# A softplus MLP in chunks of four f tiles with all tokens inside, its low weight parts on VectorE, and one gather earlier

## The chip, the cores and the metric

The kernel runs on one core of one Trainium2 chip. The metric is the device time of one execution in microseconds (us); lower is better. TensorE is called PE here, VectorE DVE, ScalarE ACT, GpSimd POOL and SyncE SP. PE runs its matmuls in order, and every engine works through its own queue in program order: the kernel is built with a manual schedule, so the order of the Python calls is the order on each engine.

## The reference

Three stages follow one another: attention in which a query sees only keys of its own hash bucket, a mixture of experts (one expert for each token), and a dense MLP with softplus. Cut to what matters:

```python
def _attn_ref(q, k, v, proj):                  # B, H, S, D = 2, 8, 768, 64
    mask = bucket(q @ proj)[..., :, None] == bucket(k @ proj)[..., None, :]
    scores = np.where(mask, scale * q @ k.T, -1e9)
    return softmax(scores) @ v

def _moe_ref(x, modality_id, w_gate, modality_bias, w1, w2):   # N, D, E, F = 1536, 512, 8, 1024
    e_idx = argmax(x @ w_gate + modality_bias[modality_id])
    for e in range(E):
        out[e_idx == e] = gate_w * (relu(x[e_idx == e] @ w1[e]) @ w2[e])

def _moe2_ref(x, w_in, w_out):                 # d_model, d_ff = 512, 2048
    h = x @ w_in
    g = np.maximum(h, 0.0) + np.log1p(np.exp(-np.abs(h)))
    return g @ w_out
```

The weights of the last stage come as 8-byte floats; they are read as pairs of 32-bit words.

## The kernel before

**Arithmetic.** Every large product is made of three matmuls on a high and a low part: xH·wH, xL·wH and xH·wL. The high part is a copy rounded to the matmul's type (made by ACT), the low part the rest (a subtraction of two tiles). So each weight tile costs one ACT copy and one subtraction.

**Experts.** `pipe` runs 16 slots of 128 tokens, each with one expert's weights. For slot s, `gather(s)` (an indirect DMA issued by POOL) fetches the rows of the slot's tokens, `xT` transposes them on PE, `g1` and `g2` are the two products, and `yout` scales the result on ACT and scatters it, with an indirect DMA of POOL's, into `x2_dram`, sorted by expert. The weight splits (`split_hi` on ACT, `split_lo` on DVE, L1000) run up to four tiles ahead of PE. `gather(1)` and `gather(2)` are issued in `route_b`, and `gather(s + 2)` for s from 1 on at the head of `pipe`'s slot s, behind the routing work that POOL has queued. The first part of the experts overlaps the end of attention by a hand-written order: `DRAIN` holds three strings of short names, one for PE, one for ACT, one for DVE and POOL, and `do` turns each name into a call (`b2` is `route_b(2)`, `Y` is `yout(0)`, `d1` is `route_d(1)`).

**Overflow.** Behind slot 16 stands a block under `tc.If` (L1206) for rare slot counts; in these runs it is not entered, and POOL settles the semaphores of the scatters that it skips.

**Second MLP.** The 2048 hidden units are 16 f tiles of 128. Weights of tile f: `wload` (two DMAs on SP into one of two buffers `wraw`), `wconv` (three DVE operations, L1276, L1278, L1280, that make 4-byte floats of the pairs), `wsplit` (high part on ACT, L1289; low part on POOL, L1290). Tokens: `x2load` brings 128 rows of `x2_dram` (from tile 4 on by SP's queue, two buffers), `x2prep` transposes them on PE (L1252) and splits them into x2H and x2L. The 12 token tiles are three groups g of four. `mlp1(g, f)` is 12 matmuls (L1301), then on ACT Abs, Exp and Ln, then on DVE gg (L1309), gH and gL (L1318). `mlp2(g, f)` is another 12 matmuls (L1336): four token tiles, three each, into four PSUM banks `ps_o`. On PE the order is mlp1 of a step, then mlp2 of the step before.

The loop in `mlp` is g outside and f inside: the 16 f tiles of group 0, in whose steps all weights are converted and split just in time (`jit`), then 16 of group 1, then 16 of group 2 with the weights kept in SBUF. PSUM sums over all f; after f = 15 each token tile is copied out (L1342 on ACT, L1344 on DVE) and scattered to the output by POOL (L1345). The token tiles of group g+1 are loaded and prepared in the last four steps of group g. The last six f of group 2 (`NLATE`) run mlp1 first and then all of mlp2 token tile by token tile, so that the output starts early. The step (0, 0), and the first weights (f = 0, 1, 2), are done inside the experts, from a hook of `pipe`: `wsplit(0)` and `wsplit(1)` behind slots 5 and 9, `wsplit(2)` and mlp1(0, 0) in the last slot.

Of the kernel before, what the change touches and what calls it, by code (L numbers as in the profile page):

```python
# [479 lines left out]
class Moe:  # L480
# [651 lines left out]
    def pipe(self, a, b, hook):  # L1132

        if a > 1:
            self.order(a, b)
            for _ in range(3):
                self.split()
            self.xT(a)
        for s in range(a, b + 1):
            if a + 2 <= s + 2 < b:  # L1140
                self.gather(s + 2)
            if s < b:
                for c in range(4):
# [71 lines left out]
    def open_mlp_early(self, ctx):  # L1215
        tc = self.tc
        kw = dict(reuse_waits="tile")
        self.wwa = ctx.enter_context(tc.tile_pool(name="wwa", bufs=1, **kw))
        self.gp = ctx.enter_context(tc.tile_pool(name="gp", bufs=2, **kw))
        self.x2_p = ctx.enter_context(tc.tile_pool(name="x2_p", bufs=2, **kw))  # L1220
        self.sA = ctx.enter_context(ExitStack())
        self.wraw = self.sA.enter_context(tc.tile_pool(name="wraw", bufs=2, **kw))
        self.mw, self.x2, self.x2t, self.oidx, self.mraw, self.m32 = {}, {}, {}, {}, {}, {}
        self.early = [0, 1, 2]
        self.NLATE = 6

    def open_mlp(self, ctx):
        kw = dict(reuse_waits="tile")
        self.wwb = ctx.enter_context(self.tc.tile_pool(name="wwb", bufs=1, side="right", **kw))
        self.po = ctx.enter_context(self.tc.tile_pool(name="po", bufs=4, space=PSUM, **kw))  # L1230

    def x2load(self, j):
        t = self.x2_p.tile([P, self.D + 1], F32, tag="x2", name="x2")
# [5 lines left out]
    def x2prep(self, j):  # L1239
        nc = self.nc  # L1240
        g, i = divmod(j, 4)
        if i == 0:
            if g == 1:
                self.sA.close()
                self.x2b = self.sA.enter_context(self.tc.tile_pool(name="x2b", bufs=1, reuse_waits="tile"))
            pool = self.x2b if g == 1 else self.x2_p
            self.x2t[g] = [pool.tile([P, self.KD, 512], F32R, tag="x2" + n, name="x2" + n, bufs=1) for n in "HL"]
        H, L = self.x2t[g]
        x = self.x2.pop(j)
        ps = self.pt.tile([P, self.KD, P], F32, tag="pt", name="ps_x2")  # L1250
        for k in range(self.KD):
            nc.tensor.transpose(ps[:, k], x[:, k * P:(k + 1) * P], self.ident)  # L1252
        sl = slice(i * P, (i + 1) * P)
        nc.scalar.copy(H[:, :, sl], ps)
        nc.vector.tensor_tensor(L[:, :, sl], ps, H[:, :, sl].bitcast(F32), op=ALU.subtract)
        if i == 0:
            self.oidx[g] = self.x2_p.tile([P, 4], I32, tag="oidx", name="oidx", bufs=3)
        (nc.vector if g == 1 and i < 2 else nc.gpsimd).tensor_copy(self.oidx[g][:, i:i + 1], x[:, self.D:])
# [24 lines left out]
    def wsplit(self, f):  # L1283
        nc = self.nc
        w = self.m32.pop(f).bitcast(F32)
        pool = self.wwa if f in self.early else self.wwb
        H = pool.tile([P, 2, 512], F32R, name=f"mwH{f}")
        L = pool.tile([P, 2, 512], F32R, name=f"mwL{f}")
        nc.scalar.copy(H, w)  # L1289
        nc.gpsimd.tensor_tensor(L, w, H.bitcast(F32), op=ALU.subtract)  # L1290
        self.mw[f] = (H, L)

    def mlp1(self, g, f):
        nc = self.nc
        H, L = self.mw[f]
        xH, xL = self.x2t[g]
        ps = self.py.tile([P, 512], F32, tag="py", name="ps_f")
        for k in range(self.KD):
            sl = slice(k * P, (k + 1) * P)
            for n, (w, x) in enumerate(((H, xH), (H, xL), (L, xH))):  # L1300
# [2 lines left out]
        nc.scalar.activation(a, ps, AF.Abs)  # L1303
        nc.scalar.activation(a, a, AF.Exp, scale=-1.0)
        nc.scalar.activation(a, a, AF.Ln, bias=1.0)  # L1305
        jit = not g and f > 0
        conv = self.wconv(f + 3, nc.vector) if jit and f + 3 < self.NF else iter(())
        gg = self.gp.tile([P, 512], F32, tag="gg", name="gg")
        nc.vector.scalar_tensor_tensor(gg, ps, 0.0, a, op0=ALU.max, op1=ALU.add)  # L1309
        late = g == self.TT // 4 - 1 and f >= self.NF - self.NLATE  # L1310
        gH, gL = (self.x2b.tile([P, 512], F32R, name=f"g{n}{f}") if late else self.gp.tile([P, 512], F32R, tag=f"g{n}", name=f"g{n}")
                  for n in "HL")
        if g:
            nc.vector.tensor_copy(gH, gg)
        else:
            nc.scalar.copy(gH, gg)
        next(conv, None)
        nc.vector.tensor_tensor(gL, gg, gH.bitcast(F32), op=ALU.subtract)  # L1318
        next(conv, None)
        if jit and f + 2 < self.NF:  # L1320
            self.wsplit(f + 2)
        next(conv, None)
        if jit and f + 5 < self.NF:
            self.wload(f + 5)
        return gH, gL

    def mlp2(self, g, f, gH, gL, tiles=range(4)):
        nc = self.nc
        H, L = self.mw[f]
        NF = self.NF  # L1330
        if f == 0:
            self.ops = [self.po.tile([P, self.D], F32, tag="po", name="ps_o") for _ in range(4)]
        for i in tiles:
            sl = slice(i * P, (i + 1) * P)
            for n, (a, w) in enumerate(((gH, H), (gH, L), (gL, H))):
                nc.tensor.matmul(self.ops[i], a[:, sl], w[:, 1], start=(f == 0 and n == 0), stop=(f == NF - 1 and n == 2))  # L1336
            if f == NF - 1:
                if i == 0:
                    self.osb = self.gp.tile([P, 4, self.D], F32, tag="osb", name="osb", bufs=1)
                o = self.osb[:, i]  # L1340
                if i % 2:
                    nc.scalar.copy(o, self.ops[i])  # L1342
                else:
                    nc.vector.tensor_copy(o, self.ops[i])  # L1344
                nc.gpsimd.indirect_dma_start(out=self.out, in_=o, in_offset=None,  # L1345
                                             out_offset=bass.IndirectOffsetOnAxis(ap=self.oidx[g][:, i:i + 1].bitcast(U32), axis=0),
                                             bounds_check=self.N - 1, oob_is_err=False)

    def mlp(self):
        NF = self.NF  # L1350
        pend = self.pend
        NG = self.TT // 4
        for g in range(NG):
            for f in range(NF):
                if g + 1 < NG:
                    if NF - 4 <= f < NF - 2:
                        self.x2load(4 * (g + 1) + f - (NF - 4))
                    elif f >= NF - 2:
                        j = 4 * (g + 1) + 2 * (f - (NF - 2))
                        self.x2prep(j)  # L1360
                        self.x2prep(j + 1)
                        if f == NF - 2:
                            self.x2load(j + 2)
                            self.x2load(j + 3)
                if g == NG - 1 and f == 0:
                    self.sA.close()
                    self.x2b = self.sA.enter_context(self.tc.tile_pool(name="late", bufs=1, reuse_waits="tile"))
                if (g, f) != (0, 0):
                    pend.append((g, f) + self.mlp1(g, f))
                if len(pend) > 1 and (g < NG - 1 or f < NF - self.NLATE + 1):  # L1370
                    self.mlp2(*pend.pop(0))

        last = [(i, x) for i in range(4) for x in pend]
        n = len(pend)
# [15 lines left out]

# [3 lines left out]
)  # L1394

# [2 lines left out]
def kernel(ctx, tc, q, k, v, proj, mid, wg, mb, w1, w2, win, wout, out):  # L1398
# [6 lines left out]
    with tc.manual_schedule():  # L1405
# [4 lines left out]
        with ExitStack() as c0:  # L1410
# [51 lines left out]
            def do(k):  # L1462
# [53 lines left out]
                    moe.hT_pe(0, *n, bank(att.ps_t, "t"))  # L1516
                elif a in "QR":
                    (moe.hT_hi if a == "Q" else moe.hT_lo)(0, *n)
                elif a == "Y":
                    moe.yout(0)  # L1520
                elif a == "z":
# [99 lines left out]
```

## Time and profile before

| | us |
|---|---|
| median of 3 runs | 782.02 (781.60 to 782.22) |
| the profiled execution, whole | 782.45 |
| its span on the core | 780.7 |
| PE busy | 756.3 (97%) |
| DVE busy | 585.2 (75%) |
| ACT busy | 520.5 (67%) |
| POOL busy | 284.0 (36%) |

Times of rows are us from the span's start. The page's busy share is an average: attention takes the first 270 us, the experts run to about 494 us, the second MLP from there to the end. The stages have to be read one by one. A matmul's shown duration overlaps that of its neighbours, so 12 matmuls of about 0.4 us each take 2.8 us, and PE's pace is better read from starts than from its busy share.

### The profile page before, as it was taken

The page shows a single profiled execution, that of the slowest core. Times are in us where ns is not written, and L with a number is a line of the kernel's source. Part 1 is how long each engine was busy: PE and PEld are TensorE (multiplying, and loading weights), DVE is VectorE, ACT ScalarE, POOL GpSimd, SP SyncE. Part 2 cuts the span into 40 slices and gives each one's busy share as a digit, 9 for nine tenths or more (in the row PEclk, how much of TensorE's full clock was granted, in tenths as well). Part 3 has the DMA queues.
Part 4 walks back from the last instruction along what each step waited for, and adds up shares of the span by engine and source line. Part 5 has one row for each costly group of instructions (what it writes and reads, how often), then busy time and mean ns, then how long its engine had stood idle before and what let it go on. Part 6 is the DMA issues. An engine that isn't in the chain of part 4 may idle for free.

```text
span 780.7 us, 13124 instructions
## 1 busy us (share of the span) xinstructions
PE 756.3 (97%) x4231; PEld 644.5 (83%) x4232; DVE 585.2 (75%) x845; ACT 520.5 (67%) x869; POOL 284.0 (36%) x624
## 2 busy tenths in 40 slices
PE   8899999999999998999999999999989999999996
PEld 6899999999999866878878878776668888888874
DVE  6898888988988797999998988799983323433250
ACT  5788787887879677898898988545554333342340
POOL 4555544446565475233342153544441100020001
PEclk9999999999999999999999999999999999999999
DMA  7845636636570014579963642334431000010001
GB/s 187 192 126 126 163 88 164 150 70 169 176 206 22 21 42 144 212 237 349 373 234 107 217 139 80 117 121 162 162 108 52 27 1 1 27 55 1 0 1 54
DMA packets 72601, 95.28 MB, mean 122 GB/s; under 512 B 31842, under 2 KB 48226, under 8 KB 72528
## 3 DMA queue, kind: packets, MB, share of 16 engines
q1 hardware_dynamic: 67152, 83.85, 36.1%
q0 software_dynamic: 3744, 9.45, 3.4%
q10 hardware_dynamic: 1632, 1.08, 0.5%
q8 instruction: 35, 0.57, 0.3%
q14 instruction: 38, 0.31, 0.1%
HBM read 105.18 MB, written 10.76 MB: 148 GB/s over the span
## 4 chain that ended last, share of the span: by engine, by line
PE 73%; DVE 9%; DMA 8%; issue 4%; POOL 3%; ACT 2%; ACTq 0%; POOLq 0%; DVEq 0%; SPq 0%
PE ps_o L1336 12%; PE ps_f L1301 12%; PE ps_o L310 9%; PE ps_y L1116 8%; PE s L253 8%; PE ps_t L286 8%; PE ps_g L1069 7%; DMA x_dram<-y,cpi 6%; DVE w L1280 3%; PE s L332 2%; DVE w L1278 2%; PE ps_prep L184 2%; PE ps_ht L1087 1%; PE ps_prep L178 1%; DVE gL L1318 1%
## 5 line engine op out<-in xcount | busy, mean ns | idle before, releaser
L1000 DVE TENSOR_TENSOR wL<-wr,wH 128x1024 fp32r<-128x1024 f32 (+1 forms) x137 | 162.7, 1218 | 13.1 <-ACT wH L995 12.8
L995 ACT CAST wH<-wr 128x1024 fp32r<-128x1024 f32 (+1 forms) x144 | 141.3, 1005 | 8.3 <-PE ps_g L1069 3.1
L1309 DVE SCALAR_TENSOR_TENSOR gg<-ps_f,ga 128x512 f32<-128x512 f32 x48 | 33.0, 688 | 108.0 <-ACT ga L1305 108.0
L263 DVE TENSOR_REDUCE mx<-s 128x1 f32<-128x768 f32 x96 | 91.5, 954 | 21.6 <-PE s L332 18.9
L274 ACT ACTIVATE p<-s,nb,sc 128x768 f32<-128x768 f32 x96 | 95.9, 999 | 15.6 <-POOL nb L265 12.8
L296 DVE TENSOR_TENSOR PL<-ps_t,PH 128x512 fp32r<-128x512 f32 x144 | 98.2, 683 | 6.8 <-ACT PH L291 6.3
L1303 ACT ACTIVATE ga<-ps_f 128x512 f32<-128x512 f32 x48 | 28.6, 597 | 108.0 <-PE ps_f L1301 107.9
L291 ACT CAST PH<-ps_t 128x512 fp32r<-128x512 f32 x144 | 83.7, 587 | 16.0 <-PE ps_t L286 13.4
L253 PE MATMUL s<-K,Q 76*128 76x384 f32 (+1 forms) x384 | 89.0, 353 | 2.4 <-ACT K L239 1.5
L310 PE MATMUL ps_o<-PH,vhl 128*128 128x256 f32 x288 | 86.8, 317 | 0.3 <-ACT Os L316 0.3
L286 PE MATMUL ps_t<-ident,p 128*128 128x128 f32 x576 | 86.3, 272 | 0.4 <-DVE PL L296 0.4
L1301 PE MATMUL ps_f<-x2H,mwL 128*128 128x512 f32 x192 | 76.7, 400 | 3.4 <-POOL mwL L1290 3.4
L1301 PE MATMUL ps_f<-x2H,mwH 128*128 128x512 f32 x192 | 76.3, 398 | 0.6 <-PEq L1206 0.6
L1336 PE MATMUL ps_o<-mwH,gL 128*128 128x512 f32 x192 | 76.8, 400 | 0.0
L1336 PE MATMUL ps_o<-mwH,gH 128*128 128x512 f32 x192 | 75.8, 395 | 0.0
L1336 PE MATMUL ps_o<-mwL,gH 128*128 128x512 f32 x192 | 75.8, 395 | 0.0
L1301 PE MATMUL ps_f<-x2L,mwH 128*128 128x512 f32 x192 | 75.5, 393 | 0.0
L286 PEld LDWEIGHTS ps_t<-ident,p 128*128 128x128 f32 x576 | 69.4, 141 | 2.3 <-PE s L253 0.7
L1290 POOL TENSOR_TENSOR mwL<-w,mwH 128x1024 fp32r<-128x1024 f32 x16 | 47.3, 2959 | 62.7 <-ACT mwH L1289 57.3
L310 PE MATMUL ps_o<-PL,vhl 128*64 128x256 f32 x288 | 68.3, 280 | 0.0
L253 PEld LDWEIGHTS s<-K,Q 76*128 76x128 f32 (+1 forms) x384 | 63.5, 191 | 4.3 <-ACT p L274 2.1
L1128 POOL DMA_INDIRECT x_dram<-y,cpi x17 | 25.1, 1476 | 100.1 <-ACT y L1123 63.2
(293 smaller groups left out, 1655.2 us busy)
## 6 DMA issues: line engine op xcount, KB each, us to landing
wr<-in_moe_w_dram SPq DMA_DIRECT2D x136, 512.0 KB
wraw<-in_moe_w_in_dram SPq DMA_DIRECT2D x16, 512.0 KB
wraw<-in_moe_w_out_dram SPq DMA_DIRECT2D x16, 512.0 KB
Q<-qH SPq DMA_DIRECT2D x28, 192.0 KB
K<-kH SPq DMA_DIRECT2D x28, 192.0 KB
rawv<-in_v_dram SPq DMA_DIRECT2D x8, 384.0 KB
x_dram<-x SPq DMA_DIRECT2D x8, 384.0 KB
rawq<-in_q_dram SPq DMA_DIRECT2D x14, 192.0 KB
```

Source lines behind the costliest of these rows:

```text
L253: self.nc.tensor.matmul(s[:, h, :HS], d[l, j][:kk, ts], d[r, j][:kk, h * HS:(h + 1) * HS], start=(a == 0), stop=(a == 1))
L263: nc.vector.tensor_reduce(mx, s[:, :, :self.HS], axis=AX.XY, op=ALU.max)
L274: self.nc.scalar.activation(e["P"][ti].rearrange("p (h c) -> p h c", h=2), s[:, :, :self.HS], AF.Exp, scale=sc, bias=nb, accum_out=e["sum" ...
L286: self.nc.tensor.transpose(ps[:, kk, t], e["P"][t][:, kt * P:(kt + 1) * P], self.ident)
L291: self.nc.scalar.copy(e["PH"][:, 2 * bk:2 * bk + 2].rearrange("p k n -> p (k n)"), e["T", bk])
L296: self.nc.vector.tensor_tensor(e["PL"][:, sl].rearrange("p k n -> p (k n)"), e["T", bk], e["PH"][:, sl].rearrange("p k n -> p (k n)").bitc ...
L310: self.nc.tensor.matmul(O[:n, :2 * P], vh[:, j, kt, :n], e[nm][:, kt], start=(kt == 0 and n == P), stop=(kt == NT - 1 and n == P))
L995: self.nc.scalar.copy(self.wt[s, c][0][:, sl], self.raw[c][:, sl])
L1000: eng.tensor_tensor(L[:, sl], self.raw[c][:, sl], H[:, sl].bitcast(F32), op=ALU.subtract)
L1116: nc.tensor.matmul(ps, a[:, f], ww[:, w], start=(f == 0 and n == 0), stop=(f == self.KF - 1 and n == 2))
L1301: nc.tensor.matmul(ps, w[:, 0, sl], x[:, k], start=(k == 0 and n == 0), stop=(k == self.KD - 1 and n == 2))
L1336: nc.tensor.matmul(self.ops[i], a[:, sl], w[:, 1], start=(f == 0 and n == 0), stop=(f == NF - 1 and n == 2))
```

## The change

It regroups the second MLP. Chunks c of four f tiles are the outer loop, the three token groups come inside, and the four f of the chunk innermost: (c, g, k). A PSUM sum now covers four f; at the end of each (c, g) the four token tiles are taken out of PSUM into an SBUF tile `acc`: by an ACT copy in chunk 0, by a DVE addition in the later chunks. The output is scattered from `acc` in the last chunk, with the 12 scatters declared free of each other. Weight tiles rotate through eight pairs of buffers. The low weight parts (`wsplit`), those of f = 0, 1 and 2 in the experts' stage too, are made by DVE in place of POOL. Within each run of 12 steps, conversions for the next chunk lie in steps 1, 2, 5 and 9 and splits in the step after each. All token tiles must be there by step 8, so their loads and preparations move to the first seven steps: tiles 4 and 5 are loaded before step 1 and prepared at the head of step 2. Four late steps stand in place of six. `gather(3)` moves from the head of slot 1 into the hand-written order, behind `b6`.

```diff
-            if a + 2 <= s + 2 < b:
+            if a + 2 <= s + 2 < b and s > 1:
                 self.gather(s + 2)
...
-    " ... Z0 l70 b5 b6 l71 j2 Y d0 d1 Z1"
+    " ... Z0 l70 b5 b6 G l71 j2 Y d0 d1 Z1"
...
+                elif a == "G":
+                    moe.gather(3)
...
+        self.acc = self.wwb.tile([P, self.TT, self.D], F32, name="acc")
...
         nc.scalar.copy(H, w)
-        nc.gpsimd.tensor_tensor(L, w, H.bitcast(F32), op=ALU.subtract)
+        nc.vector.tensor_tensor(L, w, H.bitcast(F32), op=ALU.subtract)
...
-        if g:
-            nc.vector.tensor_copy(gH, gg)
-        else:
-            nc.scalar.copy(gH, gg)
+        if then:
+            nc.scalar.copy(gH, gg)
+        else:
+            nc.vector.tensor_copy(gH, gg)
...
+            if k < self.CH - 1:
+                continue
+            acc = self.acc[:, 4 * g + i]
+            if c == 0:
+                nc.scalar.copy(acc, self.ops[i])
+            else:
+                nc.vector.tensor_tensor(acc, self.ops[i], acc, op=ALU.add)
+            if f == self.NF - 1:
+                d = nc.gpsimd.indirect_dma_start(out=self.out, in_=acc, ...)
+                self.tc.declare_no_dep(d.ins, group="out", reason="disjoint rows")
+                self.tc.add_to_no_dep_group("out", d.ins)
...
+        seq = [(g, c * CH + k) for c in range(NF // CH) for g in range(NG) for k in range(CH)]
+        self.late.update(seq[-CH:])
+        for f in range(CH, NF):
+            c, k = divmod(f, CH)
+            at = (c - 1) * NG * CH + (1, 2, 5, 9)[k]
+            conv, then = self.step.get(seq[at], ((), []))
+            self.step[seq[at]] = (f, then + [(self.wsplit, CH - 1)] * (f == CH))
+            self.step[seq[at + 1]] = ((), [(self.wsplit, f)] + [(self.wload, f + 2)] * (f + 2 < NF))
+        for n, (g, f) in enumerate(seq):
+            j = 4 + 2 * {0: 0, 2: 1, 3: 2, 5: 3}.get(n, NF)
+            if j < self.TT:
+                if n:
+                    self.x2prep(j - 2)
+                    self.x2prep(j - 1)
+                self.x2load(j)
+                self.x2load(j + 1)
+            elif n == 6:
+                self.x2prep(self.TT - 2)
+                self.x2prep(self.TT - 1)
...
+            if n:
+                pend.append((g, f) + self.mlp1(g, f))
+            if len(pend) > 1 and pend[0][:2] not in self.late:
+                self.mlp2(*pend.pop(0))
```

## Rows read from the trace of the kernel before

**Rows 1.** Chain that ended last, second MLP: start, us, what; gg in group 0's steps

```profile
551.16 0.69 DVE gg L1309
...
557.65 0.69 DVE gg L1309
```

**Rows 2.** The same chain, PE pieces after group 0, and the last mlp1 run

```profile
584.84 2.79 PE ps_f L1301 x12
...
665.51 2.81 PE ps_o L1336 x12
669.19 2.75 PE ps_f L1301 x12
...
742.34 14.40 PE ps_f L1301 x60
```

**Rows 3.** Timeline: start, us, engine, line, operation; DVE conversion with POOL idle, with POOL subtracting

```profile
447.84 1.22 DVE L1280 SCALAR_TENSOR_TENSOR w<-wraw,w 128x1024 int32<-128x1024 int32 x1
...
507.04 2.98 POOL L1290 TENSOR_TENSOR mwL<-w,mwH 128x1024 fp32r<-128x1024 f32 x1 [0.64 <-ACT mwH L1289]
507.64 3.45 DVE L1278 SCALAR_TENSOR_TENSOR w<-wraw,w 128x1024 int32<-128x1024 int32 x1
```

**Rows 4.** Timeline of PE where the second MLP's loop starts: steps 1 and 2

```profile
494.14 0.47 PE L1301 MATMUL ps_f<-x2H,mwH 128*128 128x512 f32 x1 [0.59 <-PEq L1206]
...
499.75 0.40 PE L1301 MATMUL ps_f<-x2H,mwH 128*128 128x512 f32 x1
```

**Rows 5.** Windows: stretch, us, busy PE, PEld, DVE, ACT, POOL, granted clock, DMA share, GB/s

```profile
585.00:668.00 83.00, 83.00 (x360) 67.25 (x359) 27.80 (x46) 30.08 (x49) 4.54 (x6) 1.00 0.06 20
```

**Rows 6.** Groups by line, 540 to 781 us: the copies out of PSUM on DVE

```profile
L1344 DVE COPY osb<-ps_o 128x512 f32<-128x512 f32 x6 | 3.9, 686 | 8.0 <-PE ps_o L1336 8.0
```

**Rows 7.** Timeline of PE and DVE: transposes of slot 3, the routing reduction

```profile
301.58 0.63 PE L1042 MATMUL ps_xt<-ident,xg 128*128 128x128 f32 x4 [2.37 <-DMA xg<-x_dram,idi]
...
291.13 0.32 DVE L949 TENSOR_REDUCE epr<-ep 128x21 f32<-128x168 f32 x1
```

**Rows 8.** Windows of one us behind the transposes of slot 3 (columns of Rows 5)

```profile
302.00:303.00 1.00, 1.00 (x6) 0.82 (x5) 0.13 (x1) 0.75 (x2) 0.13 (x1) 0.94 0.43 74
303.00:304.00 1.00, 1.00 (x4) 0.64 (x3) 0.74 (x2) 0.78 (x1) 0.00 (x0) 0.50 0.49 188
...
306.00:307.00 1.00, 1.00 (x6) 0.77 (x5) 0.74 (x2) 0.53 (x1) 0.00 (x0) 0.86 0.92 201
```

**Rows 9.** Timeline of POOL around `gather(3)`

```profile
289.13 0.75 POOL L938 TENSOR_TENSOR ep<-pad,es 128x168 f32<-128x168 f32 x1
...
297.24 1.95 POOL L987 DMA_INDIRECT xg<-x_dram,idi  x1 [0.16 <-issue]
```

**Rows 10.** Timeline of PE and POOL: the split of f = 0

```profile
350.98 0.72 PE L1069 MATMUL ps_g<-wL,xH 128*128 128x512 f32 x2 [0.50 <-DVE wL L1000]
...
347.10 2.74 POOL L1290 TENSOR_TENSOR mwL<-w,mwH 128x1024 fp32r<-128x1024 f32 x1 [8.68 <-ACT mwH L1289]
```

**Rows 11.** Timeline of ACT and POOL: last result tile and its scatter

```profile
493.64 0.69 ACT L1123 ACTIVATE y<-ps_y,gsl 128x512 f32<-128x512 f32 x1 [1.29 <-issue]
...
496.74 1.81 POOL L1128 DMA_INDIRECT x_dram<-y,cpi  x1 [0.28 <-POOL y L1127]
```

**Rows 12.** DMA issues, the scatter at 496.74: count, median us to landing

```profile
x_dram<-y,cpi POOLq DMA_INDIRECT x1, 5.9
```

**Rows 13.** DMA issues, the scatter at 450.02: count, median us to landing

```profile
x_dram<-y,cpi POOLq DMA_INDIRECT x1, 10.5
```

**Rows 14.** Line L1206 on POOL's sequencer: duration ns min/median/max, first and last start

```profile
L1206 POOLq INC_SWDGE_SEM  x1: 916/916/916, 502.9 to 502.9; - x1
```

**Rows 15.** Windows of one us at the join (columns of Rows 5)

```profile
502.00:503.00 1.00, 1.00 (x6) 0.79 (x6) 0.97 (x2) 0.29 (x1) 0.00 (x0) 1.00 0.51 197
```

**Rows 16.** Chain that ended last: an x2 tile's load, issue to landing

```profile
580.72 2.67 DMA x<-x_dram
```

**Rows 17.** Timeline of DVE: gH of the last step

```profile
759.53 0.43 DVE L1314 CAST gH<-gg 128x512 fp32r<-128x512 f32 x1
```

More of the change, by code (lines that the diff above doesn't have):

```diff
@@ L1223, in open_mlp_early @@
         self.mw, self.x2, self.x2t, self.oidx, self.mraw, self.m32 = {}, {}, {}, {}, {}, {}
+        self.step, self.late = {}, set()
+        self.CH = 4
         self.early = [0, 1, 2]
-        self.NLATE = 6
     def open_mlp(self, ctx):
@@ L1242, in x2prep @@
         if i == 0:
[L1243 to L1247, printed above, removed]
+            pool = self.wwb if g else self.x2_p
+            self.x2t[g] = [pool.tile([P, self.KD, 512], F32R, tag=f"x2{n}{g}", name="x2" + n, bufs=1) for n in "HL"]
         H, L = self.x2t[g]
@@ L1285, in wsplit @@
         w = self.m32.pop(f).bitcast(F32)
-        pool = self.wwa if f in self.early else self.wwb
-        H = pool.tile([P, 2, 512], F32R, name=f"mwH{f}")
-        L = pool.tile([P, 2, 512], F32R, name=f"mwL{f}")
+        n = f % (2 * self.CH)
+        pool = self.wwa if n in self.early else self.wwb
+        H = pool.tile([P, 2, 512], F32R, tag=f"mwH{n}", name=f"mwH{f}")
+        L = pool.tile([P, 2, 512], F32R, tag=f"mwL{n}", name=f"mwL{f}")
         nc.scalar.copy(H, w)
-        nc.gpsimd.tensor_tensor(L, w, H.bitcast(F32), op=ALU.subtract)
+        nc.vector.tensor_tensor(L, w, H.bitcast(F32), op=ALU.subtract)
         self.mw[f] = (H, L)
@@ L1305, in mlp1 @@
         nc.scalar.activation(a, a, AF.Ln, bias=1.0)
-        jit = not g and f > 0
-        conv = self.wconv(f + 3, nc.vector) if jit and f + 3 < self.NF else iter(())
+        conv, then = self.step.pop((g, f), ((), ()))
+        conv = self.wconv(conv, nc.vector) if conv else iter(())
         gg = self.gp.tile([P, 512], F32, tag="gg", name="gg")
         nc.vector.scalar_tensor_tensor(gg, ps, 0.0, a, op0=ALU.max, op1=ALU.add)
-        late = g == self.TT // 4 - 1 and f >= self.NF - self.NLATE
+        late = (g, f) in self.late
         gH, gL = (self.x2b.tile([P, 512], F32R, name=f"g{n}{f}") if late else self.gp.tile([P, 512], F32R, tag=f"g{n}", name=f"g{n}")
                   for n in "HL")
-        if g:
+        if then:
+            nc.scalar.copy(gH, gg)
+        else:
             nc.vector.tensor_copy(gH, gg)
-        else:
-            nc.scalar.copy(gH, gg)
         next(conv, None)
@@ L1319, in mlp1 @@
         next(conv, None)
-        if jit and f + 2 < self.NF:
-            self.wsplit(f + 2)
         next(conv, None)
-        if jit and f + 5 < self.NF:
-            self.wload(f + 5)
+        for x, k in then:
+            x(k)
         return gH, gL
@@ L1329, in mlp2 @@
         H, L = self.mw[f]
-        NF = self.NF
-        if f == 0:
+        c, k = divmod(f, self.CH)
+        if k == 0 and tiles[0] == 0:
             self.ops = [self.po.tile([P, self.D], F32, tag="po", name="ps_o") for _ in range(4)]
@@ L1335, in mlp2 @@
             for n, (a, w) in enumerate(((gH, H), (gH, L), (gL, H))):
[L1336 to L1347, printed above, removed]
+                nc.tensor.matmul(self.ops[i], a[:, sl], w[:, 1], start=(k == 0 and n == 0), stop=(k == self.CH - 1 and n == 2))
@@ new lines, in mlp2 @@
+            if k < self.CH - 1:
[6 more added lines that the diff above has]
+            if f == self.NF - 1:
+                d = nc.gpsimd.indirect_dma_start(out=self.out, in_=acc, in_offset=None,
+                                                 out_offset=bass.IndirectOffsetOnAxis(ap=self.oidx[g][:, i:i + 1].bitcast(U32), axis=0),
+                                                 bounds_check=self.N - 1, oob_is_err=False)
+                self.tc.declare_no_dep(d.ins, group="out", reason="disjoint rows")
+                self.tc.add_to_no_dep_group("out", d.ins)
@@ L1349, in mlp @@
     def mlp(self):
-        NF = self.NF
-        pend = self.pend
+        NF, CH, pend = self.NF, self.CH, self.pend
         NG = self.TT // 4
[L1353 to L1371, printed above, removed]
+        seq = [(g, c * CH + k) for c in range(NF // CH) for g in range(NG) for k in range(CH)]
@@ new lines, in mlp @@
+        self.late.update(seq[-CH:])
[16 more added lines that the diff above has]
+                self.x2prep(self.TT - 1)
+            if n == len(seq) - CH:
+                self.sA.close()
+                self.x2b = self.sA.enter_context(self.tc.tile_pool(name="late", bufs=1, reuse_waits="tile"))
+            if n:
+                pend.append((g, f) + self.mlp1(g, f))
+            if len(pend) > 1 and pend[0][:2] not in self.late:
+                self.mlp2(*pend.pop(0))
```

2 rows, old and new, of the table DRAIN are left out of this document.

## The prediction

> **What bounds the kernel now.** The first view to read is the chain of work that ended last, in order of time, because PE is busy nearly all along and only the chain tells where something else sets the pace. In the second MLP it shows two regimes. Behind 584.84 it holds PE pieces alone, 12 matmuls each: from 584.84 to 742.34 lie 56 pieces and two pairs of token transposes, and a pair takes 669.19 - 665.51 - 2.81 = 0.87 [rows 2]. So a piece takes (157.50 - 1.74) / 56 = 2.78 us, and a step (mlp1 and mlp2) 5.56. In group 0 the chain runs through DVE, and gg returns every 557.65 - 551.16 = 6.49 us [rows 1]. Next come the timelines of the engines, for why: a conversion took 1.22 with POOL idle and 3.45 beside POOL's subtraction of 2.98 [rows 3]. Group 0 is bound by DVE, and DVE by POOL.
>
> PE's loss follows by counting: from 494.14 [rows 4] to 584.84 PE does 28 pieces (mlp1 of f = 1 to 14, mlp2 of f = 0 to 13) and two pairs of transposes, 28 x 2.78 + 1.74 = 79.6 us of work in 90.7. **11.1 us are lost there**, and nearly none later. Last, PE's timeline in the experts: slot 3's transposes wait 2.37 us for a gather [rows 7], and two waits of 0.5 follow POOL's splits of f = 0 and 1 (the first is shown) [rows 10].
>
> **The gather.** It was issued at 297.24, at the end of POOL's routing work [rows 9]; PE stood still for 2.37 us until it had landed, at 301.58 [rows 7]. Then the granted clock fell from 1.00 to 0.50, from 2.4 to 1.2 GHz: 0.94, three windows at 0.50, 0.86 [rows 8]. With PE busy in all of them that is 0.06 + 1.50 + 0.14 = 1.70 us. Moved behind `b6`, the gather goes out before the y copy and `ep` (289.13), some 8 us earlier, and lands before 299.2 even at the slowest landing shown, 10.5 us [rows 13]: 4.07 us won. What is queued behind it on POOL moves by the gather's 1.95 us and a gap of 0.3 at most [rows 9]: the y copy, slot 0's scatter, `ep` and the routing up to `Mg`. DVE's reduction at 291.13 [rows 7] reads `ep`, until now ready at 289.88 [rows 9]; it then comes at 292.1, up to 1 us late, and DVE's weight splits wait behind it. PE was close behind these; I put 0.4 there (0 to 1.0). What is late next in slot 3 are the low weight parts, which DVE has done one to four tiles ahead. Net -3.7 (-4.1 to 0).
>
> **Low parts on DVE.** Each costs as much as a weight split in the experts, which is the same shape and takes 1.22 without company (DVE's conversion, also two SBUF inputs, has the same length) [rows 3]. In the slots where `wsplit(0)` and `wsplit(1)` fall, 1.22 on DVE takes the place of POOL's 2.74 [rows 10], beside which DVE's next operation was slowed by about as much. PE's two waits of 0.5 should go: -1.0 (-1.0 to +1.0).
>
> In the second MLP, 12 steps now hold four conversions and splits. DVE's share: 27.80 us in 83 of group 1's steps [rows 5], so 1.86 a step for gg, gH and gL; four tiles of four operations of at most 1.22; 12 additions at 0.69, the copy out of the same banks [rows 6]. 22.3 + 19.5 + 8.3 = 50 of 66.7 us. The fullest steps (2, 14, 26: conversion and split, gH on ACT) have 1.4 + 4.9 = 6.3 us against 5.56, and the step behind has no conversion: the excess of 0.8 is absorbed there, since no weight made there is needed before the next chunk (f = 3 alone is needed in step 3, one step after its split). POOL subtracts no more, so all conversions stand at 1.22. The 11.1 us go. The cover is DVE's 16 us of slack in 12 steps.
>
> **The PSUM hand-over.** Each (chunk, group) must empty four banks before the next fills them. After mlp1 of the new step, gH is done 759.96 - 756.74 = 3.2 us later, as at the end of the kernel [rows 2, 17], and gL at 3.9; four additions follow, at 4.6, 5.3, 6.0 and 6.7. The banks are wanted at 5.56, 6.26, 6.95, 7.65. A slack of 0.95 everywhere: 0 us. The designed free steps 0, 4 and 8 carry no conversion. In chunk 0 ACT copies; it has 5.56 - 2.0 us free a step [rows 5].
>
> **The join, a new wait.** Token tiles 4 and 5 are now transposed at the head of step 2, where PE arrives at 499.75 [rows 4]; before, that was 80 us later. Their load reads `x2_dram`, so it waits for the last scatter. That one was issued at 496.74 behind POOL's split of f = 2, though y was ready at 493.64 + 0.69 = 494.33 [rows 11]; it landed 5.9 us later [rows 12], and then POOL needed 0.92 us to settle the skipped block's semaphores, from 502.9 [rows 14]. With that split on DVE the scatter goes out at about 495.0. I take 4 us for its landing (2.67, the landing of a plain load [rows 16], to 5.9), as the weight load of f = 5, whose data fill the DMA up to the middle of the window at 502 [rows 15], comes behind it. So: 499.0, settled by 500.1, x2 load 2.67 [rows 16], 502.8, second tile 0.3 later. The load stands on SP behind the weight load of f = 5 as well, which bounds the start from below at about 502. Behind the waiting transposes stand mlp1(0, 2) and all of PE's queue. PE stands still for 3.4 us (2.3 to 9.7, the latter with the landing of 10.5 [rows 13]), and as 2.37 us of standing still brought the clock down [rows 8], I add the same 1.7. **+5.1** (0 if the tiles come in time, at most 11.4). The next pairs have a whole step (5.56) for a load of 2.67 and its issue: nothing.
>
> Rows 3 show DVE slowed by POOL; the other way round, the scatter of 10.5 us shows a scatter of POOL's late, while DVE was splitting weights. The Trainium skill (SBUF — State Buffer, section "SBUF: two separate sides") says that a DMA issued by POOL can starve because DVE locks POOL out of a shared port, and (section "Who interferes with whom") that a subtraction of two SBUF tiles should take only the port's read side. By the first the join would cost up to 11.4, by the second 5.1; the trace does not separate them.
>
> **The end.** Four late f in place of six: the last f is wanted after four products of a quarter piece, 2.78 us, but its gH takes 3.2 and its gL 0.7 more: +0.7. Five mlp1 in a row took 14.40 against 13.9 [rows 2]; three should lose 0.2, not 0.5. The last copy (ACT) becomes an addition of 0.69 [rows 6], +0.1. Net +0.5 (0 to 1.5). The scatters' mutual waits were worth nothing before, when token tiles ended 18 matmuls, 4.2 us, apart and a scatter landed in 5.9 at most on a busy DMA; 0, and 0 to -1 in the range.
>
> **Sum.** -3.7 - 1.0 - 11.1 + 5.1 + 0.5 = -10.2. Against the profiled execution's own 782.45 that is 772.2; that execution lay 0.4 above the median of the runs, so I forecast 782.02 - 10.2 = **771.8**.
>
> **Rivals.** (B) The x2 rows come much later: scatter landing in 10.5, stall 9.7: 771.8 + 6.3 = 778.1. For it: one scatter in the experts did so [rows 13]. Against: DVE has only two operations queued at that moment. (C) No stall: 766.7. For it, only if the scatter lands in less than the shortest row; against, the chain of three waits. (D) The gather brings nothing, because DVE's low parts are late in slot 3 instead: 775.5. For it, DVE is nearly full there and delayed by `ep`; against, it waited for PE's transposes in that stall. (E) Slower: the hand-over. With nine groups of additions, eight of them waited for, each must cost PE 1.5 us to undo 10.2 and 1.6 more; as the slack is 0.95 for four additions, that decides from an addition of 1.3 us (0.69 + (0.95 + 1.5) / 4). At 1.4 us the time would be 771.8 + 8 x 1.9 = 787. Against: the copy out of the same banks takes 0.69. (F) The change does not relieve DVE: conversions stay at 3.45 without POOL. Then the full steps hold some 10 us, but only the first ones are wanted soon: +3 us, 774.8.
>
> **How the numbers follow.** Forecast 0.54 (own range 769.5 to 774.5); B 0.17; C 0.10; D and F 0.12; E 0.04; B and D together, about no change, 0.03. The range goes from C to B: 766.5 to 778.5. A measurement of this kernel tells 0.2% (1.6 us) from no change. Faster 0.93, same 0.03, slower 0.04.
>
> **What would show it.** In the changed kernel: no wait at slot 3's transposes and a clock of 1.00 there; no subtraction L on POOL and conversions of 1.22; steps of 5.56 from step 3 to the end; one PE wait of 2 to 5 us at the first x2 transposes behind step 1, for a DMA, with the clock at 0.50 behind it; additions of 0.69 with no PE wait at chunk heads; a wait below 1 us for the last gH. I am wrong if x2 pairs wait again and again, if PE waits at the hand-overs, or if the clock stays low for longer than three windows.

## The result, and the profile after

The changed kernel takes 771.84 us (median of 4 runs, 769.36 to 773.32) where the kernel before, run beside it, took 781.86: a ratio of 0.987, 95% interval 0.984 to 0.990. Forecast were 771.8. Repeated later (e5 below) it gave 0.987 again (0.984 to 0.990), 10.9 us under before. The median of before differs a little between the three groups of runs below (780.06, 781.51, 781.54), so every number is compared with the run of before in its own group. In one profiled execution of all, that of the last experiment, PE took 2.6 times as long for the same work (7.17 us for 12 matmuls); only POOL's spacing is read from it.

The profiled execution took 769.36, 767.6 of it the span. The page's busy times and the chain's shares by engine:

```profile
PE 748.5 (98%) x4232; PEld 646.6 (84%) x4232; DVE 596.5 (78%) x894; ACT 522.3 (68%) x872; POOL 227.9 (30%) x608
...
PE 91%; POOL 2%; DVE 2%; issue 2%; DMA 1%; ACT 1%; POOLq 0%; ACTq 0%; SPq 0%; DVEq 0%
```

PE alone now carries the chain. In the second MLP that was DVE's part before [rows 1]. DVE's groups by line (busy us, mean ns of one | idle before):

```profile
L1280 DVE SCALAR_TENSOR_TENSOR w<-wraw,w 128x1024 int32<-128x1024 int32 x16 | 19.6, 1227 | 0.4
L1291 DVE TENSOR_TENSOR mwL<-w,mwH 128x1024 fp32r<-128x1024 f32 x16 | 19.6, 1222 | 2.3 <-ACT mwH L1290 2.3
...
L1342 DVE TENSOR_TENSOR acc<-ps_o,acc 128x512 f32<-128x512 f32 x36 | 22.6, 683 | 6.2 <-PE ps_o L1335 6.2
```

Every conversion (L1278 like L1280) stands at 1.22 where [rows 3] had up to 3.45, the low part costs the same, and an addition 0.68. The chain (start, us, what) where the loop starts, and its pieces at the end:

```profile
487.29 0.70 ACT y L1123
...
488.73 3.40 DMA x_dram<-y,cpi
...
492.20 4.21 DMA x<-x_dram
...
504.19 2.79 PE ps_f L1302 x12
...
739.68 5.48 PE ps_f L1302 x24
...
751.41 8.60 PE ps_o L1335 x35
```

Behind one wait, told by the chain of scatter (its 3.40 includes POOL's settling of the skipped block), x2 load and first transposes, every piece takes 2.7 to 2.8 us: from 504.19 to 739.68 lie 84 pieces and two pairs of transposes, (235.49 - 1.74) / 84 = 2.78, and a step is 5.57. The timelines of POOL, PE and DVE at slot 3, at the join and at the end (in square brackets the wait and what ended it):

```profile
287.17 1.13 POOL L987 DMA_INDIRECT xg<-x_dram,idi  x1 [0.60 <-issue]
290.17 0.75 POOL L938 TENSOR_TENSOR ep<-pad,es 128x168 f32<-128x168 f32 x1
...
294.84 0.74 PE L1069 MATMUL ps_g<-wL,xH 128*128 128x512 f32 x2 [1.02 <-DVE wL L1000]
299.10 0.60 PE L1042 MATMUL ps_xt<-ident,xg 128*128 128x128 f32 x4
...
496.55 1.23 PE L1252 MATMUL ps_x<-ident,x 128*128 128x128 f32 x8 [2.94 <-DMA x<-x_dram]
...
740.67 2.48 DVE L1342 TENSOR_TENSOR acc<-ps_o,acc 128x512 f32<-128x512 f32 x4
751.41 0.50 PE L1335 MATMUL ps_o<-mwH,gH 128*128 128x512 f32 x1 [0.41 <-DVE gH L1317]
```

Two windows of one us, behind slot 3's transposes and behind those at the join (columns of [rows 5]; the granted clock is the third number from the end):

```profile
303.00:304.00 1.00, 1.00 (x8) 0.88 (x7) 0.98 (x2) 0.71 (x3) 0.00 (x0) 1.00 0.65 217
...
498.00:499.00 1.00, 1.00 (x6) 0.80 (x5) 1.00 (x3) 0.41 (x1) 0.00 (x0) 1.00 0.00 0
```

Slot 3's transposes wait no more [rows 7] and the clock stays at 1.00 there (in [rows 8] it was 0.50). What is new are 1.02 at 294.84, 2.94 at the join, 0.41 at the last gH, and four additions in a row at a hand-over, for which PE does not wait.

### The profile page after: what moved, and what is told of

Same layout as the page of the kernel before. It is cut to its first block, busy times and chain, and to the rows that moved or that the text cites. A ratio compares the mean times of both kernels' runs of the same rounds, so it can differ in the third digit from the quotient of the medians.

```text
span 767.6 us, 13126 instructions
## 1 busy us (share of the span) xinstructions
PE 748.5 (98%) x4232; PEld 646.6 (84%) x4232; DVE 596.5 (78%) x894; ACT 522.3 (68%) x872; POOL 227.9 (30%) x608
## 4 chain that ended last, share of the span: by engine, by line
PE 91%; POOL 2%; DVE 2%; issue 2%; DMA 1%; ACT 1%; POOLq 0%; ACTq 0%; SPq 0%; DVEq 0%
PE ps_f L1302 17%; PE ps_o L1335 17%; PE ps_y L1116 11%; PE ps_g L1069 10%; PE ps_o L310 9%; PE s L253 9%; PE ps_t L286 8%; PE s L332 2%; PE ps_prep L184 2%; PE ps_ht L1087 2%; PE ps_prep L178 2%; PE ps_xt L1042 1%; PE ps_x L1252 1%; DMA x<-x_dram 1%; POOL xg L987 1%
## 5 line engine op out<-in xcount | busy, mean ns | idle before, releaser
L274 ACT ACTIVATE p<-s,nb,sc 128x768 f32<-128x768 f32 x96 | 95.9, 999 | 15.9 <-POOL nb L265 13.1
L1344 POOL DMA_INDIRECT out_dram<-acc,oidx x12 | 11.7, 972 | 231.0 <-DVE acc L1342 227.9
L1128 POOL DMA_INDIRECT x_dram<-y,cpi x17 | 19.0, 1118 | 125.9 <-ACT y L1123 89.6
```

The lines of the kernel that those rows point to most:

```text
L274: self.nc.scalar.activation(e["P"][ti].rearrange("p (h c) -> p h c", h=2), s[:, :, :self.HS], AF.Exp, scale=sc, bias=nb, accum_out=e["sum" ...
```

## The experiments

**Theory.** The time comes from two places: PE's stall for the gather (3.4 to 4), and DVE relieved of POOL's company in group 0 (11), and the new order gives part of it back at the join. **Rivals:** that the chunks themselves, by spreading the conversions, bring the gain; that the gain at the gather is given back; that the hand-over costs something all along.

**e1_gather_back.** The changed kernel, with `gather(3)` where it was.

```diff
-            if a + 2 <= s + 2 < b and s > 1:
+            if a + 2 <= s + 2 < b:
                 self.gather(s + 2)
...
-    " ... Z0 l70 b5 b6 G l71 j2 Y d0 d1 Z1"
+    " ... Z0 l70 b5 b6 l71 j2 Y d0 d1 Z1"
```

> The changed kernel with the gather of slot 3 back at the head of slot 1. My theory (the gather's wait at slot 3 and the slow clock behind it were worth 3.4 to 4.1 us): 775 to 776 against the changed kernel's 771.8, with PE waiting 1.3 to 2.4 us at slot 3's transposes. Rival D (the gather brought nothing, the gain is in the second MLP alone): within 0.7 us of 771.8.

Measured: 773.89, 6.2 under before (0.991, interval 0.988 to 0.994); the change stood 10.0 and 10.9 under its own runs of before, so the gather is worth 3.8 to 4.7. PE's timeline, and one window in each of the two low stretches (the clock is the third number from the end):

```profile
301.47 0.63 PE L1042 MATMUL ps_xt<-ident,xg 128*128 128x128 f32 x4 [2.33 <-DMA xg<-x_dram,idi]
...
303.00:304.00 1.00, 1.00 (x4) 0.61 (x4) 0.75 (x2) 0.67 (x1) 0.00 (x0) 0.50 0.49 188
...
500.54 1.73 PE L1252 MATMUL ps_x<-ident,x 128*128 128x128 f32 x7 [3.10 <-DMA x<-x_dram]
...
502.00:503.00 1.00, 1.00 (x5) 0.90 (x4) 0.97 (x3) 0.79 (x2) 0.00 (x0) 0.50 0.08 16
```

Stall and clock are back with the gather's old place: the mechanism is shown. The clock fell at the join as well in this execution.

**e2_low_parts_only.** The kernel before with one line changed.

```diff
-        nc.gpsimd.tensor_tensor(L, w, H.bitcast(F32), op=ALU.subtract)
+        nc.vector.tensor_tensor(L, w, H.bitcast(F32), op=ALU.subtract)
```

> The kernel before with one line changed: the low weight parts of the second MLP made by DVE in place of POOL; order of the second MLP, gather and scatters as before. Theory 1 (POOL's subtraction slowed DVE's conversions and that alone made group 0 slow): group 0's steps fall from 6.49 to about 5.57 us, the two waits of 0.5 us in the experts go, and the time is 782 - 11 - 1.6 = 769 to 770, under the changed kernel although it holds no chunk. Theory 2 (the just-in-time weights need the spreading over three groups): DVE keeps group 0 above 6 us a step, and the time is 776 or more.

Measured: 768.41, 11.7 under before (0.984, 0.981 to 0.987), though slot 3 still waits 2.42. Its chain in group 0, the window of four steps there (columns of [rows 5]), and DVE's groups by line:

```profile
542.71 2.79 PE ps_f L1301 x12
545.50 2.79 PE ps_o L1336 x12
...
537.00:559.50 22.50, 22.50 (x98) 18.18 (x97) 21.74 (x26) 13.87 (x21) 0.00 (x0) 1.00 0.62 211
...
L1278 DVE SCALAR_TENSOR_TENSOR w<-wraw,w 128x1024 int32<-128x1024 int32 x16 | 19.6, 1225 | 0.0
L1290 DVE TENSOR_TENSOR mwL<-w,mwH 128x1024 fp32r<-128x1024 f32 x16 | 19.5, 1219 | 0.5 <-ACT mwH L1289 0.5
```

Steps of 5.58 with a conversion and a split in each: DVE is busy 21.74 of 22.50 us, 97%, and still keeps PE's pace once POOL is silent. **One line brings as much as the whole change or more.**

**e7_chunks_pool_low.** The other half alone: the changed kernel with that line on POOL again (the diff of e2 the other way round).

> The changed kernel with the low weight parts back on POOL, in its chunked order. Theory (chunks and DVE's low parts are two cures for one loss, group 0's; either alone takes most of it away): steps of 5.57 us from step 4 on in spite of conversions of 2 to 3.5 us, as they are spread over three groups; lost against the changed kernel are the two waits of 0.5 in the experts (1.6 with what hangs on them) and a later last scatter (1.6 us at the join): 3 to 4 us above the changed kernel. Rival (the low parts carry the gain alone, the chunks none): 8 to 11 us above it, near the kernel before.

Measured: 775.28 (0.9925, 0.990 to 0.995), 6.2 under before and 4.7 above the change run beside it. POOL and DVE at the join, PE's wait there, and the chain later:

```profile
510.05 3.12 POOL L1291 TENSOR_TENSOR mwL<-w,mwH 128x1024 fp32r<-128x1024 f32 x1 [9.44 <-ACT mwH L1290]
510.92 3.33 DVE L1280 SCALAR_TENSOR_TENSOR w<-wraw,w 128x1024 int32<-128x1024 int32 x1
...
500.22 1.90 PE L1252 MATMUL ps_x<-ident,x 128*128 128x128 f32 x8 [4.26 <-DMA x<-x_dram]
...
547.97 2.76 PE ps_o L1335 x12
550.73 2.81 PE ps_f L1302 x12
```

The chunks alone also reach 5.57 a step: with one conversion in three steps, DVE can afford one of 3.33. So the two are **two cures for one loss**, and only one is needed. The 4.7 lie at the join (PE waits 4.26 in place of 2.94, and 0.46 for x2L at 515.50) and in the experts, where the two waits of 0.5, at 347.66 and 397.84, and the slowed split beside each are back (0.8 a piece, below): 1.3 + 0.5 + 1.6 = 3.4. The remaining 1.3 may be the clock: in this execution it fell to 0.50 behind the wait of 4.26, which costs 1.7, and behind the change's own wait it fell in some executions only. How often it falls in either kernel, these runs do not tell.

**e6_old_order_all_else.** Therefore the kernel before with the line of e2 and the earlier gather, and the old order.

> The kernel before, its old order of the second MLP and its scatters, with the low weight parts on DVE and the gather moved up: the change without the chunks. Theory 1 (the chunks add nothing to the gain and cost the join): the gains add up, 11.7 us (low parts alone) and 3.4 to 4.1 (gather), so 15 us under the kernel before and 4 to 5 under the changed kernel. Theory 2 (the chunks give part of the gain, or the gather's gain is lost to something later in this order): 10 to 12 us under the kernel before.

Measured: 766.07 (0.981, 0.9785 to 0.983), 15.4 under before and **4.5 faster than the change** run beside it. Its chain in group 0 and at the end:

```profile
551.95 2.79 PE ps_o L1336 x12
554.74 2.79 PE ps_f L1301 x12
...
739.88 16.82 PE ps_o L1336 x72
```

From loop start to PE's last product it takes 756.70 - 487.74 = 269.0, the change 760.0 - 487.87 = 272.1: the 2.94 of the join and 0.2 besides. Of the rest of the 4.5, 0.4 is the tail behind that product (7.6 in the change, 7.2 here); the other 0.9 may be the clock in the executions where it falls, which no row here separates.

**e3_fill_the_wait.** The changed kernel with twelve matmuls of no use ahead of the transposes of token tile 4, their result overwritten.

```diff
+        if j == 4:
+            for _ in range(12):
+                nc.tensor.matmul(ps.rearrange(...), self.mw[0][0][:, 0, :P], self.x2t[0][0][:, 0], ...)
```

> The changed kernel with 12 further matmuls on PE (their result is overwritten, nothing reads it) in front of the transposes of token tile 4, where PE stands still for 2.94 us. Theory (the spread of the changed kernel's runs, 769.4 to 773.3, is the clock that falls behind this wait in some executions and not in others): all executions come to 769.3 to 770.0, since the filler takes 2.8 us in place of the wait and the clock has no reason to fall there. Rival (the spread comes from elsewhere, as from the attention stage): the same spread of 2 to 4 us, median about 772.

Measured: 770.07 (769.52 to 771.01; 0.987, 0.984 to 0.990). In the profiled execution PE waits 0.20 at the transposes, and its clock stays at 1.00. The median is not clearly below the change; the spread is 1.5 where the change has 4.0 and 3.5. **Half settled:** with the stall filled the clock did not fall there, but that the stall makes the spread is not shown. The kernel of e9 below has no stall at the join and spreads by 3.0 (765.33 to 768.32); in its slowest run, the profiled one, the clock fell at 34 us, in attention.

**e4_prepare_later.** The changed kernel with four x2 buffers in place of two: tiles 4 to 7 loaded ahead of step 1, tiles 4 and 5 transposed behind step 2's mlp1, the others at steps 3, 5 and 6.

```diff
-        t = self.x2_p.tile([P, self.D + 1], F32, tag="x2", name="x2")
+        t = self.x2_p.tile([P, self.D + 1], F32, tag="x2", name="x2", bufs=4)
...
+        if (g, f) == (0, 2):
+            self.x2prep(4)
+            self.x2prep(5)
...
+            if n in (3, 5, 6):
+                j = {3: 6, 5: 8, 6: 10}[n]
+                self.x2prep(j)
+                self.x2prep(j + 1)
+            for j in {0: range(4, 8), 3: range(8, 12)}.get(n, ()):
                 self.x2load(j)
```

> The changed kernel with the wait taken away: four x2 buffers in place of two, token tiles 4 to 7 all loaded before step 1, and tiles 4 and 5 transposed behind mlp1(0, 2) in place of ahead of it, so PE comes there 2.8 us later. Theory (the join costs 2.94 us and in most executions a slow clock on top): PE's wait falls under 0.5 us, and all executions come to 766.0 to 767.5. Rival (the wait is passed on to tiles 6 and 7, or DVE is late in steps 2 to 4): a new wait of 1 to 3 us in steps 3 and 4, 768 to 770.

Measured: 768.16 (0.984, 0.981 to 0.987), 11.9 under before. The chain at the join:

```profile
493.59 2.81 PE ps_f L1302 x12
...
496.43 0.64 PE ps_x L1252 x4
...
497.70 2.74 PE ps_o L1338 x12
```

The join's wait is gone. The gain over the change is 1.0 by the difference to before (11.9 against 10.9) and 1.9 against its other runs (10.0), less than the 2.9 of the wait: the theory had asked for more. By the rows, from loop start to PE's last product it takes 757.69 - 487.80 = 269.9, 2.2 less than the change.

**e5_after_again.** The changed kernel once more, on the chip of e6 and e7.

> The changed kernel itself, to stand beside the others of this call on the same chip: 10.0 us under the kernel before, as in its first measurement, with executions spread over some 4 us. Where PE waits about 3 us at the first x2 transposes, the clock falls behind it in some executions and not in others.

Measured: 770.57 (0.987, 0.984 to 0.990). Its join, PE's timeline and three windows:

```profile
496.48 1.79 PE L1252 MATMUL ps_x<-ident,x 128*128 128x128 f32 x8 [2.75 <-DMA x<-x_dram]
...
496.00:497.00 1.00, 0.53 (x4) 0.56 (x4) 0.97 (x2) 0.00 (x0) 0.00 (x0) 0.83 0.16 60
497.00:498.00 1.00, 1.00 (x7) 0.93 (x6) 1.00 (x2) 0.49 (x1) 0.00 (x0) 0.50 0.00 0
...
500.00:501.00 1.00, 1.00 (x5) 0.82 (x5) 0.00 (x0) 0.00 (x0) 0.00 (x0) 0.97 0.66 166
```

Here the clock fell behind 2.75 us of standing still (0.17 x 1 + 3 x 0.5 + 0.03 = 1.7 us lost), where the first profile, behind 2.94, had 1.00.

**e8_additions_doubled.** Rival E of the prediction: each addition gets a DVE copy out of the same bank ahead of it.

```diff
+                nc.vector.tensor_copy(self.gp.tile([P, self.D], F32, tag="twice", ...), self.ops[i])
                 nc.vector.tensor_tensor(acc, self.ops[i], acc, op=ALU.add)
```

> The changed kernel with a further DVE copy out of the same PSUM bank in front of each of the 32 additions. The additions take 2.48 us for four (0.62 each in a row); with the copies eight operations take about 5.0. Theory (the hand-over of the four banks has 0.95 us of slack, as worked out before): the last bank is free at about 3.9 + 5.0 = 8.9 us behind the step's mlp1 and wanted at 7.65, so PE waits some 1.2 us at each of eight hand-overs, 9 to 10 us in all. Rival (more slack than that): no wait at the hand-overs, time unchanged.

Measured (one run): 783.52, 2.0 above the run of before beside it and 13 above the change. The chain at one hand-over:

```profile
588.63 0.68 DVE twice L1342
...
591.70 0.61 DVE acc L1343
592.35 0.96 PE ps_o L1335 x3
```

At 0.68 + 0.61 = 1.29 us a bank the additions are in the chain; at 0.68 they are not. By the prediction's slack of 0.95 this costs 4 x (1.29 - 0.69) - 0.95 = 1.45 at each of eight hand-overs, 11.6; 13 were measured. By the rows PE's stretch from loop start to its last product is 773.91 - 488.90 = 285.0, 12.9 more than in the change's first profile; 1.7 of that is the clock, which fell at the join here and not there, and 11.2 are left. So the slack is there, and rival E's edge with it.

**e9_old_order_gather_behind_ep and e11_old_order_again.** e6 with the gather directly behind `ep`, and e6 once more beside it.

```diff
             G.tensor_tensor(self.ep, self.pad[:, E:2 * E].unsqueeze(1).to_broadcast([P, NX, E]), self.es, op=ALU.mult)
+            self.gather(3)
             for _ in self.gate3(G, NT, TT):
...
-    " ... Z0 l70 b5 b6 G l71 j2 Y d0 d1 Z1"
+    " ... Z0 l70 b5 b6 l71 j2 Y d0 d1 Z1"
```

> The old order of the second MLP with low parts on VectorE (as in e6_old_order_all_else), and the early gather issued right behind ep instead of ahead of it. Theory (the gather of 1.1 us ahead of ep holds ep up, with it DVE's reduction and the weight split behind, and costs PE the wait of 1.0 us at 294.9): that wait is 0.2 again as before the change, slot 3 still has no wait and full clock, since the gather goes out some 2 us later and still lands before 299; 0.8 us below the old order with the gather ahead of ep, some 16.2 us under before. Rival (the wait of 1.0 has another cause, or the time is given back at the next wait of the experts): within 0.2 us of it. Second rival: the gather lands after 299 and PE waits there again, up to 4 us slower.

> The same kernel as e6_old_order_all_else, on the chip of this call, so that the two gather places and the two orders are compared on one chip: 15.4 us under before, ratio 0.981.

Measured: 765.88 (0.979, 0.9775 to 0.981) and 765.76 (0.980, 0.978 to 0.982): no difference. POOL and PE of e9:

```profile
290.34 0.75 POOL L938 TENSOR_TENSOR ep<-pad,es 128x168 f32<-128x168 f32 x1
291.25 2.14 POOL L988 DMA_INDIRECT xg<-x_dram,idi  x1 [0.16 <-issue]
...
296.67 2.32 POOL L943 TENSOR_TENSOR Mg<-so,g 128x756 bf16<-128x756 bf16 x1
...
299.05 0.54 PE L959 MATMUL psg<-Mg,Rt 128*128 128x63 bf16 x12 [0.95 <-POOL Mg L943]
```

The wait for wL of 1.02 is gone, and one of 0.95 for `Mg` has taken its place: the gather now takes 2.14 on POOL, not 1.13, and what is behind it comes late. My theory fell; the rival held. PE is close behind POOL's routing there, and the gather costs it 0.8 to 0.95 on either side of `ep`.

**e10_prepare_later_gather_behind_ep.** e4 with the same place of the gather.

> The changed kernel with token tiles 4 and 5 transposed one step later and 6 to 11 later as well (as in e4_prepare_later), and the gather right behind ep. Theory 1 (the join and the end are all that the chunk order costs): 0.8 us below e4_prepare_later, some 12.7 us under before, and still 2 to 4 us above the old order run beside it, because of what the end costs and of what is left of the preparation's waits. Rival (chunk order is as good as the old order once the join is mended): within 1 us of the old order run beside it, some 15.5 us under before.

Measured: 767.76 (0.983, 0.9805 to 0.985), 2.0 above the old order beside it. Mended at the join, the chunk order is still the slower one. By the traces its loop takes 0.6 longer (269.9 from 488.41 against 269.3; the last gH is waited for with 0.4), and its tail behind PE 0.4 longer; the last 0.7 had arisen ahead of the loop and is not put down to it.

**e12_scatters_wait.** The changed kernel without the two lines that declare the output scatters free of each other.

```diff
-                self.tc.declare_no_dep(d.ins, group="out", reason="disjoint rows")
-                self.tc.add_to_no_dep_group("out", d.ins)
```

> The changed kernel with the output scatters' mutual waits back (the two lines that declare them free taken out). The prediction's term is 0, between 0 and +1. Token tiles end one piece, 2.8 us, apart at the end of the chunk order, and a scatter takes 1 us to issue and some 2.5 to 3 to land, so the waiting scatters fall behind by under 1 us each: theory 1, up to 2 us above the changed kernel (10.4 us under before becomes 8.5 to 10.4), with POOL waiting for the scatter before, and the last scatter going out late. Rival (a scatter lands before the next token tile ends): no difference that can be measured.

Measured: 776.71 (0.9935, 0.991 to 0.996), 4.8 under before, so 5 to 6 above the change. POOL's timeline, the second to the fourth scatter of four whose data were there early (the first row's wait is put down to an addition, but that one had ended at 1842.99):

```profile
1846.16 0.97 POOL L1344 DMA_INDIRECT out_dram<-acc,oidx  x1 [2.52 <-DVE acc L1342]
1849.78 0.97 POOL L1344 DMA_INDIRECT out_dram<-acc,oidx  x1 [2.65 <-DMA out_dram<-acc,oidx]
1853.37 0.97 POOL L1344 DMA_INDIRECT out_dram<-acc,oidx  x1 [2.62 <-DMA out_dram<-acc,oidx]
```

A waiting scatter goes out 3.5 to 3.6 us behind the one before. In the change the last four go out at 754.13, 756.23, 759.03 and 761.83, over 7.70 us, the later token tiles 2.79 apart; with waits the three steps would take 10.5 to 10.8, an estimate of 2.8 to 3.1 us more where up to 2 were expected. The other 2 to 3 are **not settled**. The granted clock of these runs was 0.989 to 0.992, of the change's 0.992 to 0.998; the difference of the means, 0.004, makes 0.004 x 775 = 3 us of full-speed time, but no trace shows where it was lost, nor that the waits caused it. Some of such a difference can cost nothing: in e2 the clock stood at 0.50 from 764 to 768, where PE's last product had ended at 761.3.

## Why the prediction was right

**The sum** was -10.2, and -10.0 and -10.9 were measured. Its terms one by one:

- **The gather, -3.7.** Slot 3's g1 starts at 304.75 in place of 308.86 (below: the two rows of the chain, and the wait of 0.21 before). Of these 4.1 us 0.75 are from before 287 (the same transposes begin at 286.60 and 287.36), where nothing was changed. That leaves 3.4; the runs e1 and e2 against e6 say 3.8 (15.4 - 11.7 = 3.8) to 4.7. The delay of `ep` was put at 0.4 (0 to 1.0) and is 0.8, from a wait of 0.21 to 1.02.

```profile
308.86 5.49 PE ps_g L1069 x24
...
304.75 5.49 PE ps_g L1069 x24
...
294.77 0.73 PE L1069 MATMUL ps_g<-wL,xH 128*128 128x512 f32 x2 [0.21 <-DVE wL L1000]
```

- **Low parts in the experts, -1.0.** The pieces behind f = 0 and f = 1 gain 0.8 each (354.13 and 403.50 against 359.02 and 409.23), so -1.6: outside the stated range of -1.0 to +1.0, by 0.6. The prediction counted the two waits of 0.5, and these were only what showed on PE.
- **Group 0, -11.1.** e2 holds this term and the one above: 11.1 + 1.0 = 12.1 forecast, 11.7 measured. The reason was right too: the conversions stand at 1.22. By the rows alone it is a little less: the work that took the kernel before 90.7 us takes e2 572.58 - 492.41 = 80.2, so 10.5.
- **The join, +5.1.** Waits of 2.75 to 2.94 for the forecast 3.4, and 1.7 of clock in some executions. The path was the one predicted, its terms not quite: the scatter went out 0.7 behind the end of y, as forecast; it landed in 2.3 (4 taken), and POOL's settling took 0.92 from 491.3 on, as forecast, so the load went out 3.5 behind the scatter in place of 5.1 (the chain's piece of 3.40 holds both, landing and settling); and the load took 4.2 where [rows 16] had 2.67 (3.0 with the second tile). The errors cancel: the rows were forecast 8.8 behind the end of y, and came 8.4 behind it. [rows 13]'s landing of 10.5, rival B, did not come. The forecast had the clock at 0.50 behind this wait in every execution; the first profile has 1.00 there. The scatter's landing and the settling, after:

```profile
x_dram<-y,cpi POOLq DMA_INDIRECT x1, 2.3
...
L1206 POOLq INC_SWDGE_SEM  x1: 916/916/916, 491.3 to 491.3; - x1
```

- **The hand-over, 0.** Right: no PE wait at any chunk head, and e8 shows the edge near 1.3 that rival E named.
- **The end, +0.5.** 0.41 for gH, and a tail 0.4 longer: +0.8.
- **The scatters, 0.** Read from the kernel before, where token tiles ended 4.2 apart, this was right for what was taken out (a waiting scatter needs 3.5 to 3.6 by e12), though a landing of 5.9, as the prediction took it, is longer than 4.2 and would not have given nothing. It was not right for the new order: there, where they end 2.79 apart, the waits would cost 2.8 to 3.1 by POOL's spacing (5 to 6 by the runs). The lines are needed because of the other edits.

**How the terms add up.** Between the two profiles lie 13.1 us, 0.75 of them from before 287. The rest, by rows: the gather -3.4, the experts -1.6, another -0.5 ahead of the loop, not forecast, group 0 -10.5, the join and the last gH +3.2, the tail +0.4, together -12.4. That execution kept its clock at the join; one in which it falls there is 1.7 longer, -10.7. So the mechanism was right, and that the sum came within 0.2 to 0.7 is in part luck: group 0 gave 0.6 less than forecast and the experts 0.6 more, and the clock's 1.7, put into every execution, is paid in some.

**What it did not ask.** The prediction priced the new order by its costs alone (join, end) and credited the 11.1 to the subtraction's move, which was right; it never asked what the order was then needed for. Its own rows would have told. In a step of group 0 in the old order DVE has L1276 (0.69), three operations of 1.22, gg and gL: 0.69 + 3 x 1.22 + 2 x 0.69 = 5.73 us as shown, beside PE's 5.56, and shown durations overlap by some 0.07 (four additions in a row take 2.48, one alone 0.69). That is too near to dismiss the old order, and e2's window has it at 97%.

**POOL beside DVE.** In e7 DVE's conversion begins at 510.92, POOL's subtraction ends at 513.17, and the conversion ends at 514.25, 1.1 us later; in [rows 3] likewise, 511.09 against 510.02. By these times DVE stood still nearly until POOL was done: it ended 1.1 us behind POOL, where alone it takes 1.22. The Trainium skill (SBUF — State Buffer, section "SBUF: two separate sides") states this as a rule: the port pair that the two share is a lock held for a whole instruction, and a DVE operation with two SBUF inputs is shut out by a POOL operation that reads SBUF and began first. The traces agree: in both cases POOL began first, and the conversion ended 1.1 us behind it. The starving scatter by which the prediction weighed the join did not show there: it landed in 2.3, though DVE was in a conversion of 1.23 (from 488.86) while POOL issued it.

## What to carry to other kernels

Two edits that each cure the same loss are worth it once: try each alone before building both. Here one line on another engine did what a new loop order was built for, and the order only added a wait for the last scatter of the stage before and a dearer end. The best version measured keeps the old order, makes the low parts on DVE and issues the gather early: 765.8 to 766.1, 0.980 of before (0.978 to 0.982). When work is moved forward on a queue, look at what is close behind it on the same queue: the gather cost 0.8 to 0.95 us on either side of `ep`, by another wait each time. And a dependency that costs nothing in one order (tiles 4.2 us apart) can cost in another (2.79 apart).

## What was not expected of the hardware

The granted clock behind a standstill of the same kind differed between executions: at the join it fell to 0.50 (1.2 GHz) behind waits of 2.75 (e5), 2.79 (e8), 3.10 (e1) and 4.26 (e7), and stayed at 1.00 (2.4 GHz) behind 2.94 in the first profile of the change; at slot 3 it fell behind 2.33 (e1), 2.37 (before) and 2.42 (e2). A fall cost 1.7 us, worked out at slot 3 from [rows 8] and at the join from e5. The change's eight runs go with the mean granted clock: 772.6 to 773.3 at 0.992, 771.1 at 0.994, 769.4 to 770.8 at 0.996 and above. But the mean does not tell where the clock fell: at 0.996 the first profile has a fall at 13 to 17 us, in attention, and none at the join, and e5's, at 0.996 too, has none at 13 to 17 and one at the join. A scatter issued by POOL took 1.0 us to issue and 2.5 to 2.65 more until the next, which waits for it, could go (e12).
